# A fused attention and mixture kernel: low parts of second weights on VectorE, three decoded pieces moved into the second mixture, and loads put in another order

## The chip, the cores and the metric

The kernel runs on one core of one Trainium2 chip. The metric is the device time of one execution in microseconds (us). The kernel before took 853.97 us, the median of 3 runs (851.84 to 854.99). The core has five engines with a queue of instructions each: PE (TensorE, matrix products), DVE (VectorE), ACT (ScalarE), POOL (GpSimd) and SP (SyncE, which here only issues DMAs). An instruction waits at the head of its queue until all that it needs is there, and everything behind it in the same queue waits with it.

## The reference

```python
def _attn_ref(q, k, v, beta):                 # 4 batches, 8 heads, 768 tokens, 48 wide
    k_n = k / (np.linalg.norm(k, axis=-1, keepdims=True) + 1e-06)
    state = zeros(B, H, D, D)
    for t in range(S):
        y[:, :, t] = einsum('bhd,bhde->bhe', q[:, :, t], state)
        v_old = einsum('bhde,bhd->bhe', state, k_n[:, :, t])
        state = state + bt * einsum('bhd,bhe->bhde', k_n[:, :, t], vt - v_old)

def _moe_ref(x, w_gate, w_output_gate, w1, w2):   # 3072 tokens, 384 wide, 8 experts of 1024
    e_idx = argmax(x @ w_gate); gate_w = softmax(x @ w_gate)[e_idx]
    eom = 1 / (1 + exp(-(x @ w_output_gate)))
    for e in range(8):
        out[mask] = gate_w * eom[:, e] * (maximum(x[mask] @ w1[e], 0) @ w2[e])

def _moe2_ref(x, w1, w2, w3, w_out):              # hidden width 768
    return maximum(maximum(x @ w1, x @ w2), x @ w3) @ w_out
```

The attention's output is the first mixture's input, and the first mixture's output that of the second.

## The kernel before

**Attention.** The 768 tokens of a sequence go in 24 steps of 32. A step needs the inverse of a triangular 32x32 matrix for each batch and head. Inverses are made by DVE for four steps at a time, six sets in all, by row updates (`inv_step`: a product at L239 and a sum at L245 for each of two halves); `inv_n1` to `inv_n3` prepare a set (square norms, ACT's logarithm and exponentials, DVE's reciprocal at L216, POOL's product of Z at L218), `inv_end` and `inv_store` write it to memory as `td`. In each step the chain then loads the inverse T (`loadT`, L302, the tile TT) and the keys and values (`load32`, L294, the tile kv), POOL scales the values (`vscale`, L308), and PE multiplies (L340 pU, L360 pS). The output x is stored to `xd` (L384). Step by step the tokens' experts are also found, counted (L433 cum) and written as lists into `tab` by POOL's scatters (`r_s`, L474). All of it is written out by hand in one order; times in steps such as `s.RT`, `s.RD` and `s.LT` say between which steps units of loading are put.

**First mixture.** Ten runs, each with the tokens of one expert: runs 0 to 3 of 256 tokens (experts 0 and 1 in parts), runs 4 to 9 of 440, 416, 404, 388, 380 and 368. A run gathers token rows by POOL (`gather`, L837) through a list `ids` (L821), transposes them on PE (`xpose`, L852), multiplies by the first weight (`m1`, tile ph), takes the maximum with zero on ACT (L888), multiplies by the second weight (`o1`, tile po) and stores y into `x2` (L904). `place` (L829) copies a run's list into one list `ctab`. Every product in full precision is three products of high and low parts: `mm3` (L864) of the weight's, tokens' or hidden values' high part (a cast on ACT) and low part (value less high part: L856, L889). For a weight, loaded by `raws` (L679), `split` makes the casts (L695) and the low parts (L696); its last argument is the engine of the low parts, DVE (V) or POOL (G). A first weight is split in three pieces of 128x1024, a second weight in four of 128x768. In a run k from 3 to 8 the next expert's weights are split.

**Second mixture's weights.** They come as 24 pieces of 384 columns of 64-bit words, in six for each of the four weights, the output weight last. Decode (`units`) loads a piece (L600), ACT squares (L606), DVE makes high and low parts in seven steps (L607 to L613), and SP stores them (L603) into `wd`; `load_parts(n)` (L704) loads a whole weight's parts. `pieces` chains the units so that a piece's load is issued within the piece before and its store within the piece behind it; `NP` says how many pieces a run takes.

**Second mixture.** Six blocks of 512 tokens: `m2f` (tile pm) makes three products and their maximum (L937) for each sixth of the hidden width, `o2` (tile pz) the output, which POOL scatters to its place (L950).

**Order.** In `run` each unit has a due time as a share of a run; they are sorted by it and issued in that order, which fixes every engine's queue. `s.values` reads 17 numbers of the table into SP's registers (L804), 15 for starts and experts and 2 for `s.st`, the starts of run 2's and 3's lists.

Of the kernel before, what the change touches and what calls it, by code (L numbers as in the profile page):

```python
# [8 lines left out]
F32 = mybir.dt.float32  # L9
F32R = mybir.dt.float32r  # L10
BF16 = mybir.dt.bfloat16
I32 = mybir.dt.int32
# [21 lines left out]
class Attn:  # L34
# [9 lines left out]
    def __init__(s, ctx, tc, psum, big, hp, gp, kqt, knv, bt, wgt, xd, tab, ctab, cum, ident, wrm, x2):  # L44
        s.tc, s.nc, s.psum, s.big, s.hp, s.gp = tc, tc.nc, psum, big, hp, gp
        nc = tc.nc
        s.kqt, s.knv, s.btd, s.wgtd, s.xd, s.tab, s.ctab, s.cum = kqt, knv, bt, wgt, xd, tab, ctab, cum
        s.ident, s.wrm, s.ones, s.x2 = ident, wrm, wrm[:, 0:128], x2
        s.NI = 24
        s.NP = 12  # L50
        s.NSL = 6
        s.RLB = "m"
        s.XB, s.xTs, s.RLK = 1, {}, 0
        s.CUT = 0.95
        s.NL = 4
        s.NA = 20
        s.LATE = 0.4
        s.W = (0, 1, 0)
        s.END = 13
        s.TU, s.TB, s.MF = (22.92, 22.95, 22.97), "TRT", 2  # L60

        s.BUD = (5.0, 5.6, 4.6, 5.0)

        s.ORD = {0: 0, 1: 14, 2: 36, 3: 50, 4: 66, 5: 80}
        s.prep = (2.8, 2.2, 1.5, 0.6)
        cp = s.cp = ctx.enter_context(tc.tile_pool(name="acst", bufs=1))
        s.p2 = ctx.enter_context(tc.tile_pool(name="ap2", bufs=2))
        s.dr = ctx.enter_context(tc.tile_pool(name="adr", bufs=1, space=DRAM))
        nc.scalar.preload_act_table_set("natural_log_exp_and_others")
        s.chain = False  # L70
        s.RT, s.RD, s.LT = (15.4, (15.9, 0.3), (17.4, 0.35), (20.7, 0.25)), 0.5, ((18.2, 0.45), (19.3, 0.35), (23.0, 0.05))
        s.KQT, s.AT, s.Gd, s.kv, s.TT, s.x, s.inv = {}, {}, {}, {}, {}, {}, {}

    def consts(s):
# [413 lines left out]
    def run(s, pre, tail):  # L488
# [12 lines left out]
        s1 = s.ORD[1]  # L501
        for f in merge(B[:s1 // 3], [A[4], A[5]]) + merge(B[s1 // 3:s1 // 2], [A[6], A[7]]):
            f()
        s.inv_load(1)
        for f in (s.inv_n1, s.inv_n2, s.inv_n3):
            f(1)
        for f in merge(B[s1 // 2:], [A[8], lambda: s.load32(0), A[9], s.empty, A[10], lambda: s.load32(1), A[11], lambda: s.inv_load(2)] + A[12:s.NA]):
            f()
        s.inv_end(0)
        s.warm(8, s.inv[0]["tt"])  # L510
# [114 lines left out]
class Moe:  # L625
# [179 lines left out]
                                skip_runtime_bounds_check_because="the tables keep them in range")  # L805

    def values(s):
        s.at = [0] + [s.value(s.irow, 24 + k, 0, COLS - r.n) for k, r in enumerate(s.runs) if k]
        s.ex |= {2 + k: s.value(s.irow, 34 + k, 0, 7) for k in range(6)}
        s.st = [s.value(s.irow, 40 + k, 0, s.PART) for k in range(2)]  # L810

    def start(s, r):

# [262 lines left out]
        a.r_p(q)  # L1076
        m(7)

    NP = {2: 2, 3: 2, 4: 4, 5: 4, 6: 4, 7: 4, 8: 4}

    def pieces(s):

        N = s.dec.N
        rd = [s.work[:, j * 2 * N:(j + 1) * 2 * N] for j in range(2)]
        wd = [s.work[:, (j + 1) * 4 * N:(j + 2) * 4 * N] for j in range(2)]
        u = [s.dec.units(rd[j % 2], wd[j % 2]) for j in range(len(s.dec.pieces))]
        out = []
        for j, (ld, us, st) in enumerate(u):
            nxt = [u[j + 1][0]] if j + 1 < len(u) else []
            prev = [u[j - 1][2]] if j else []  # L1090
            out.append(([ld] if j == 0 else []) + us[:2] + nxt + us[2:4] + prev + us[4:] + ([] if nxt else [st]))
        return out

    def run(s, a):
        nc = s.nc
        A, V, G = nc.scalar, nc.vector, nc.gpsimd
        s.raw = [s.p.tile([128, 3072], F32, name=f"raw{n}") for n in range(2)]
        s.work = s.p.tile([128, 12 * s.dec.N], I32, name="work")
        pieces = s.pieces()
        last = len(s.runs) - 1  # L1100
# [10 lines left out]
        for k, r in enumerate(s.runs):  # L1111

            us = []
            o = [lambda c=c: s.o1(k, c) for c in range(3)]
            x = [lambda c=c: s.xpose(k + 1, c) for c in range(3)] if k < last else []
            if k == 0:
                us += [(0, load(1, 1)), (0, lambda: a.r_s(range(4)))]
                us += [(0.01, lambda: s.xtiles(1, "1")), (0.02, x[0]), (0.2, o[0]), (0.3, x[1]), (0.5, o[1]), (0.6, x[2]), (0.7, o[2])]
                us += [(0.01, lambda: s.count(24)), (0.3, s.table), (0.4, s.table2), (0.65, s.table3), (0.8, s.values), (0.85, lambda: (s.ids(2), s.ids(3))), (0.9, lambda: rows(2))]
            else:  # L1120
                us += spread([lambda f=f: s.m1(k, f) for f in range(8)], 0, 0.5)
                us += list(zip((0.51, 0.65, 0.82), o))
                if k < last:
                    us += [(0.495, lambda: s.xtiles(k + 1, f"{k + 1}"))] + list(zip((0.5, 0.52, 0.66) if k > 1 else (0.66, 0.83, 0.84), x))
            if k == 1:
                us += spread(s.split(1, 1, A, V), 0.05, 0.4)
                us += [(-0.01, lambda: [s.ids(j) for j in range(4, 10)])]
            if k:

                free = [j for j in range(len(s.rowsets) - 6) if max(s.rowsets[j][0] - 1, 1) == k]  # L1130
                for j in free:
                    t = 0.0 if s.rowsets[j][0] < 2 else 0.845 if k == 1 else 0.665
                    us += [(t, lambda n=s.rowsets[j + 6]: s.gather(*n))]
            if k == 1:
                us += [(0.4, load(2, 0)), (0.5, pieces[0].pop(0))]
            if 3 <= k < last:
                us += spread(s.split(k - 1, 0, A, V), 0.05, 0.35) + spread(s.split(k - 1, 1, A, G), 0.5, 1)
                if k < last - 1:
                    us += [(0.6, load(k, 0))]
            if 4 <= k < last or k == 2:  # L1140
                us += [(0.15, load(max(k - 1, 2), 1))]
            if 2 <= k < last:
                us += [(0.02, lambda j=j: s.place(j)) for j in ({2: [0, 1, 2], 3: [3]}.get(k, [k]))]
                d = []
                for _ in range(s.NP.get(k, 0)):
                    d += pieces.pop(0)
                us += spread(d, 0.0, 1)
            if k == last - 1:
                us += [(0.51, lambda: s.load_parts(0))]
            if k == last:  # L1150
                us += [(0, lambda: s.place(last)), (0.01, lambda: s.load2(0)), (0.02, lambda: s.load_parts(1))]
                us += [(0.5, lambda: s.load2(1)), (0.505, lambda: s.load_parts(2))]
                us += spread([lambda c=c: s.split2(0, c) for c in range(3)], 0.6, 0.9)
            for _, u in sorted(us, key=lambda u: u[0]):
                u()
            s.ystore(k)
        s.load_parts(3)
        for b in range(6):
            us = [lambda f=f: s.m2f(b, f) for f in range(6)]
            if b < 5:  # L1160
                us += [lambda c=c: s.split2(b + 1, c) for c in range(3)]
            for u in us:
# [99 lines left out]
```

## Time and profile before

| | |
|---|---|
| median of 3 runs | 853.97 us (851.84 to 854.99) |
| profiled execution, own time | 854.27 us |
| its span | 852.6 us |
| PE busy | 746.0 us, 87% of the span |
| DVE busy | 479.7 us, 56% |
| ACT busy | 297.8 us, 35% |
| POOL busy | 279.3 us, 33% |
| DMA | 110.28 MB, 129 GB/s in the mean |

The profile is one execution. Busy shares are means over stages with different limits, so they are to be read by stage: the prologue (to about 70 us), the attention chain (to about 283), the ten runs of the first mixture (from 279 to 542, runs 4 to 9 from 369) and the second mixture (to 847). In the rows, "start us, us, engine line op out<-in xcount" is a time from the span's start, a duration, and a count of equal instructions grouped into one row; the brackets at the end say how long the engine was idle just before and what ended that. SPq and POOLq are these engines' own queues, where an issue that waits is shown as one wait. PEclk is the granted clock of TensorE, 1.00 being the higher of its two levels (2.4 GHz) and 0.50 the lower (1.2 GHz).

### The profile page before, as it was taken

The page shows a single profiled execution, that of the slowest core. Times are in us where ns is not written, and L with a number is a line of the kernel's source. Part 1 is how long each engine was busy: PE and PEld are TensorE (multiplying, and loading weights), DVE is VectorE, ACT ScalarE, POOL GpSimd, SP SyncE. Part 2 cuts the span into 40 slices and gives each one's busy share as a digit, 9 for nine tenths or more (in the row PEclk, how much of TensorE's full clock was granted, in tenths as well). Part 3 has the DMA queues.
Part 4 walks back from the last instruction along what each step waited for, and adds up shares of the span by engine and source line. Part 5 has one row for each costly group of instructions (what it writes and reads, how often), then busy time and mean ns, then how long its engine had stood idle before and what let it go on. Part 6 is the DMA issues. An engine that isn't in the chain of part 4 may idle for free. (4 is left out here: it accounts for less than half of the span.)

```text
span 852.6 us, 20332 instructions
## 1 busy us (share of the span) xinstructions
PE 746.0 (87%) x8506; PEld 635.6 (75%) x8517; DVE 479.7 (56%) x1140; ACT 297.8 (35%) x675; POOL 279.3 (33%) x346
## 2 busy tenths in 40 slices
PE   6656877778774897999999999999999999999996
PEld 4544554555552896989899889889888898988886
DVE  3898989985543453688889996132331323223130
ACT  2213576664331332454455353212121121212111
POOL 5766456522575631165455322001001010100101
PEclk7557799999786998999999999999999999999998
DMA  8795544547616126667887684901001020000001
GB/s 233 168 231 128 142 120 121 101 133 184 179 21 171 65 72 190 206 209 246 256 272 254 240 300 164 400 22 56 18 16 60 1 75 1 28 10 1 37 1 40
DMA packets 85756, 110.28 MB, mean 129 GB/s; under 512 B 53860, under 2 KB 67115, under 8 KB 82971
## 3 DMA queue, kind: packets, MB, share of 16 engines
q1 hardware_dynamic: 57259, 87.08, 32.9%
q10 hardware_dynamic: 19360, 11.42, 5.7%
q0 software_dynamic: 9040, 10.42, 4.1%
q8 instruction: 69, 1.13, 0.6%
q14 instruction: 28, 0.23, 0.1%
HBM read 79.53 MB, written 29.36 MB: 128 GB/s over the span
## 5 line engine op out<-in xcount | busy, mean ns | idle before, releaser
L864 PE MATMUL pm<-xhm,wm 128*128 128x512 f32 x648 | 204.9, 396 | 1.4 <-DMA wm<-wd 1.4
L937 DVE TENSOR_TENSOR work<-work,pm 128x512 f32<-128x512 f32 x72 | 49.5, 688 | 186.5 <-PE pm L864 186.5
L864 PEld LDWEIGHTS pm<-xhm,wm 128*128 128x128 f32 x648 | 121.9, 188 | 30.7 <-DMA wm<-wd 1.9
L864 PE MATMUL pm<-xlm,wm 128*128 128x512 f32 x324 | 128.2, 396 | 0.0
L950 POOL DMA_INDIRECT out_dram<-work,idm x24 | 23.7, 986 | 303.3 <-ACT work L949 289.0
L939 ACT CAST hmh<-work 128x512 fp32r<-128x512 f32 x36 | 22.4, 622 | 155.8 <-DVE work L937 155.8
L239 DVE TENSOR_TENSOR zt<-Z 128x30 f32<-128x30 f32 (+14 forms) x219 | 74.3, 378 | 3.2 <-POOL Z L218 2.6
L864 PE MATMUL pz<-wm,hmh 128*128 128x384 f32 x320 | 73.7, 334 | 0.0
L864 PEld LDWEIGHTS pm<-xlm,wm 128*128 128x128 f32 x324 | 61.0, 188 | 14.3
L348 ACT COPY Ubd<-pU 32x192 f32<-32x192 f32 x148 | 45.8, 309 | 66.4 <-PE pU L340 63.5
L245 DVE TENSOR_TENSOR Z<-Z,zt 128x30 f32<-128x30 f32 (+14 forms) x219 | 66.2, 342 | 0.0
L164 PE MATMUL pg<-KQT 48*32 48x64 f32 x1536 | 40.3, 293 | 21.6 <-DMA KQT<-in_kqt_dram 17.6
L837 POOL DMA_INDIRECT xg<-xd,ids x32 | 44.4, 1387 | 44.5 <-PE pt L852 29.0
L360 PE MATMUL pS<-Ubd,kv 128*48 128x192 f32 x368 | 44.2, 378 | 16.6 <-ACT Ubd L348 12.1
L864 PEld LDWEIGHTS pz<-wm,hmh 128*128 128x128 f32 x320 | 57.2, 188 | 0.5
L164 PEld LDWEIGHTS pg<-KQT 48*32 48x32 f32 x1536 | 34.5, 152 | 28.5 <-issue 15.8
L360 PEld LDWEIGHTS pS<-Ubd,kv 128*48 128x48 f32 x368 | 24.5, 140 | 36.7 <-ACT Ubd L348 23.3
L367 ACT COPY Sbd<-pS 48x384 f32<-48x384 f32 x72 | 34.0, 472 | 14.2 <-PE pS L360 13.1
L899 ACT COPY y<-po 128x256 f32<-128x256 f32 (+6 forms) x30 | 13.3, 443 | 72.3 <-PE po L864 72.3
L864 PE MATMUL pz<-wm,hml 128*128 128x384 f32 x112 | 37.4, 334 | 0.0
L308 POOL TENSOR_TENSOR kv<-kv,TT 128x384 f32<-128x384 f32 x20 | 20.8, 1040 | 46.1 <-DMA TT<-td 23.7
L888 ACT ACTIVATE hh<-ph 128x440 fp32r<-128x440 f32 (+5 forms) x48 | 24.0, 502 | 33.9 <-PE ph L864 33.6
(303 smaller groups left out, 1664.3 us busy)
## 6 DMA issues: line engine op xcount, KB each, us to landing
raw<-in_w_dram SPq DMA_DIRECT2D x13, 1536.0 KB, 10.6
kv<-in_knv_dram SPq DMA_DIRECT2D x24, 384.0 KB, 4.6
wd<-work SPq DMA_DIRECT2D x24, 384.0 KB, 5.1
wm<-wd SPq DMA_DIRECT2D x8, 1152.0 KB, 7.9
KQT<-in_kqt_dram ACTq DMA_DIRECT2D x20, 448.0 KB, 4.8
xd<-x SPq DMA_DIRECT2D x24, 192.0 KB, 5.1
r<-in_w_dram SPq DMA_DIRECT2D x9, 512.0 KB, 7.0
raw<-x SPq DMA_DIRECT2D x6, 768.0 KB, 4.9
```

The lines of the kernel that those rows point to most:

```text
L164: nc.tensor.matmul(ps[b * 32:b * 32 + 32, o:o + 64], kq[:, 0, :], kq.rearrange("p k t -> p (k t)"), start=True, stop=True, tile_position=( ...
L239: nc.vector.tensor_mul(t, Z[:, a:e, m].unsqueeze(2).to_broadcast([128, e - a, n]), Z[:, m, m + 1:].unsqueeze(1).to_broadcast([128, e - a, n]))
L245: nc.vector.tensor_add(Z[:, a:e, m + 1:], Z[:, a:e, m + 1:], t)
L348: nc.scalar.copy(dst, src)
L360: nc.tensor.matmul(s.pS[q][j * 64:j * 64 + 48, g2 * 192:g2 * 192 + 192], s.kv[i][:, 0, h, :], s.Ubd[h // 4][:, h % 4, :], start=(i == 0 an ...
L367: nc.scalar.copy(dst, src)
L837: s.nc.gpsimd.indirect_dma_start(t[0:r.ct], None, s.xd[0:2049] if k < 2 else s.xd, bass.IndirectOffsetOnAxis(s.gid[k][0:r.ct, c, 0:1], 0))
L864: s.nc.tensor.matmul(ps, a, b, start=(start and k == 0), stop=(stop and k == n - 1))
L888: nc.scalar.activation(hi, ps, AF.Relu)
L937: nc.vector.tensor_max(m, m, ps)
L939: nc.scalar.copy(hi, m)
L950: nc.gpsimd.indirect_dma_start(s.out, bass.IndirectOffsetOnAxis(i[:, c, 2:3], 0), y, None, bounds_check=3071, oob_is_err=False)
```

## The change

1. In runs 3 to 8 the low parts of the second weight, four of 128x768 in each, are made by DVE instead of POOL (`split(k - 1, 1, A, V)`).
2. The time from which the third weight (the first weight of expert 1) is loaded is 21.8 steps instead of 20.7 (`s.RT`).
3. Runs 5, 6 and 7 decode three pieces instead of four. The last three pieces, all of the output weight, are loaded into the raw weights' tiles and decoded in the first block of the second mixture, one behind each of its first three sixths; the output weight's load (`load_parts(3)`) is issued after the third.
4. In the prologue the preparation of inverse 1 is merged with steps 7 to 13 of inverse 0, so that the reciprocal stands behind step 13 instead of ahead of step 8; products A[8] and A[9] come ahead of its ACT part, and the load of kv for step 1 and the filling of the lists (`empty`) come later.
5. The load of the second weight of expert 1 (`raws(1, 1)`) is three DMAs of 128x1024 instead of one of 128x3072.
6. `values` is cut in two: two register loads, then the lists of runs 2 and 3, then the other fifteen.
7. The first piece's load is issued ahead of run 1's other units instead of in its middle.

```diff
-        s.RT, ... = (15.4, (15.9, 0.3), (17.4, 0.35), (20.7, 0.25)), ...
+        s.RT, ... = (15.4, (15.9, 0.3), (17.4, 0.35), (21.8, 0.25)), ...
...
-        for f in (s.inv_n1, s.inv_n2, s.inv_n3):
-            f(1)
-        for f in merge(B[s1 // 2:], [A[8], lambda: s.load32(0), A[9], s.empty, A[10], lambda: s.load32(1), A[11], lambda: s.inv_load(2)] + A[12:s.NA]):
+        s.inv_n1(1)
+        for f in merge(B[s1 // 2:s1], [A[8], A[9], lambda: s.inv_n2(1), A[10], lambda: s.inv_n3(1)]):
+            f()
+        for f in merge(B[s1:], [lambda: s.load32(0), A[11], lambda: s.inv_load(2), s.empty, lambda: s.load32(1)] + A[12:s.NA]):
             f()
...
     def values(s):
+        s.st = [s.value(s.irow, 40 + k, 0, s.PART) for k in range(2)]
+
+    def values2(s):
         s.at = [0] + [s.value(s.irow, 24 + k, 0, COLS - r.n) for k, r in enumerate(s.runs) if k]
         s.ex |= {2 + k: s.value(s.irow, 34 + k, 0, 7) for k in range(6)}
-        s.st = [s.value(s.irow, 40 + k, 0, s.PART) for k in range(2)]
...
-    NP = {2: 2, 3: 2, 4: 4, 5: 4, 6: 4, 7: 4, 8: 4}
+    NP = {2: 2, 3: 2, 4: 4, 5: 3, 6: 3, 7: 3, 8: 4}
...
-        u = [s.dec.units(rd[j % 2], wd[j % 2]) for j in range(len(s.dec.pieces))]
+        rl = [s.rawi[j][:, 1536:1536 + 2 * N] for j in range(2)]
+        m = sum(s.NP.values())
+        u = [s.dec.units((rd if j < m else rl)[j % 2], wd[j % 2] if j < m else s.work[:, 2560:2560 + 4 * N])
+             for j in range(len(s.dec.pieces))]
...
-            out.append(([ld] if j == 0 else []) + us[:2] + nxt + us[2:4] + prev + us[4:] + ([] if nxt else [st]))
+            out.append(([ld] if j == 0 else []) + (prev if j == m else []) + us[:2] + nxt + us[2:4] + (prev if j < m else []) + us[4:] + ([st] if j >= m else []))
...
-                us += [(0, load(1, 1)), (0, lambda: a.r_s(range(4)))]
+                us += [(0, lambda: [u() for u in s.raws(1, 1, lambda: s.raw[1], 3)]), (0, lambda: a.r_s(range(4)))]
...
-                us += [... (0.8, s.values), (0.85, lambda: (s.ids(2), s.ids(3))), (0.9, lambda: rows(2))]
+                us += [... (0.8, s.values), (0.85, lambda: (s.ids(2), s.ids(3), s.values2())), (0.9, lambda: rows(2))]
...
-                us += [(0.4, load(2, 0)), (0.5, pieces[0].pop(0))]
+                us += [(-0.02, pieces[0].pop(0)), (0.4, load(2, 0))]
...
-                us += spread(s.split(k - 1, 0, A, V), 0.05, 0.35) + spread(s.split(k - 1, 1, A, G), 0.5, 1)
+                us += spread(s.split(k - 1, 0, A, V), 0.05, 0.35) + spread(s.split(k - 1, 1, A, V), 0.5, 1)
...
-        s.load_parts(3)
         for b in range(6):
             us = [lambda f=f: s.m2f(b, f) for f in range(6)]
+            if b == 0:
+                w = [u for p in pieces for u in [lambda p=p: [f() for f in p]]]
+                us = [u for j in range(6) for u in [us[j]] + w[j:j + 1] + ([lambda: s.load_parts(3)] if j == len(w) - 1 else [])]
```

PE's queue holds the same 3413 rows in the same order as before. Line numbers of the changed kernel are up to nine higher.

In SP's queue at the end of the chain, before (r_1 is the third weight, TT and kv belong to the last steps, ids are the lists of runs 0 and 1):

```order
L679 DMA r_1_4598<-in_w_dram 128x1024
L384 DMA xd<-x_4507 128x384
L679 ISA
L679 DMA r_1_4598<-in_w_dram 128x1024
L302 DMA TT_4646<-td_173 128x8x33
L294 DMA kv_4649<-in_knv_dram 128x768
L821 ISA
L821 DMA ids_4711<-tab 128x2x3
```

The same stretch of SP's queue now:

```order
L384 DMA xd<-x_4507 128x384
L302 DMA TT_4643<-td_173 128x8x33
L294 DMA kv_4646<-in_knv_dram 128x768
L824 ISA
L824 DMA ids_4708<-tab 128x2x3
L824 ISA
L824 DMA ids_4710<-tab 128x2x3
L384 DMA xd<-x_4626 128x384
L680 ISA
L680 DMA r_1_4769<-in_w_dram 128x1024
L302 DMA TT_4795<-td_173 128x8x33
L680 ISA
```

All loads of the third weight now stand behind the TT and kv of one more step and behind both lists; the last step's TT is between the first and the second of them.

In SP's queue at the end of run 1 and the start of run 2, before (raw_5232 is the first weight of expert 2, work<-in_ma a piece's load):

```order
L821 DMA ids_5440<-tab 92x4x3
L679 ISA
L679 DMA raw_5232<-in_w_dram 128x3072
L600 DMA work<-in_ma_dram 128x768
L904 REGISTER_ALU
L904 DMA x_77<-y_5591 384x1x256
L829 ISA
L829 DMA ctab<-tab 16x48
```

The same place now, from the end of run 0's store on:

```order
L907 DMA x_77<-y_5277 384x1x256
L601 DMA work<-in_ma_dram 128x768
L824 ISA
L824 DMA ids_5433<-tab 110x4x3
...
L680 DMA raw_5232<-in_w_dram 128x3072
L907 REGISTER_ALU
L907 DMA x_77<-y_5593 384x1x256
...
L832 DMA ctab<-tab 16x48
L601 DMA work<-in_ma_dram 128x768
L680 ISA
```

The first piece's load moved ahead of six list loads and the raw weight; the second piece's, the last DMA but one shown, stays behind the copies into ctab.

In DVE's queue in the second half of run 4 (xl are the low parts of run 5's tokens, work the decode, w_3l the low parts of the second weight of expert 3), before:

```order
L856 TENSOR_TENSOR xl_6287<-pt_0_6288,xh_6286 128x416
L856 TENSOR_TENSOR xl_6287<-pt_1_6327,xh_6286 128x416
L607 TENSOR_SCALAR work<-work 128x384
L608 SCALAR_TENSOR_TENSOR work<-work 128x384
L609 SCALAR_TENSOR_TENSOR work<-work 128x384
L610 TENSOR_SCALAR work<-work 128x384
```

And now:

```order
L859 TENSOR_TENSOR xl_6289<-pt_0_6290,xh_6288 128x416
L697 TENSOR_TENSOR w_3l<-raw_5233,w_3h 128x768
L859 TENSOR_TENSOR xl_6289<-pt_1_6329,xh_6288 128x416
L608 TENSOR_SCALAR work<-work 128x384
L609 SCALAR_TENSOR_TENSOR work<-work 128x384
L610 SCALAR_TENSOR_TENSOR work<-work 128x384
L697 TENSOR_TENSOR w_3l<-raw_5233,w_3h 128x768
```

The four low parts of a second weight now stand among the tokens' low parts and the decode steps of DVE.

## Rows read from the trace of the kernel before

**Rows 1.** Busy us of each engine in two stretches, with granted clock, DMA share, GB/s:
```profile
371.00:542.00 171.00, 164.18 (x915) 156.92 (x915) 144.06 (x221) 78.00 (x138) 70.14 (x38) 1.00 0.76 252
542.00:853.00 311.00, 302.52 (x1408) 258.05 (x1406) 83.47 (x123) 65.74 (x112) 23.67 (x24) 0.99 0.12 41
```
**Rows 2.** Timeline of DVE in the prologue (start, duration, instruction, idle before):
```profile
32.12 0.35 DVE L216 RECIPROCAL vt<-vt 128x32 f32<-128x32 f32 x1 [2.30 <-POOL vt L207]
32.39 0.35 DVE L239 TENSOR_TENSOR zt<-Z 128x92 f32<-128x92 f32 x2
...
33.15 2.47 DVE L239 TENSOR_TENSOR zt<-Z 128x110 f32<-128x110 f32 x2
```
**Rows 3.** Timeline of POOL in the prologue:
```profile
32.92 2.40 POOL L218 TENSOR_TENSOR Z<-Z,vnw 128x1024 f32<-128x1024 f32 x1
```
**Rows 4.** Waits of the queue SP, 230 to 292 us (total, times, longest):
```profile
SPq L679 <- POOL w_0l L696: 20.0, 1, 20.0
```
**Rows 5.** Timeline of POOL at the end of the chain:
```profile
255.29 1.81 POOL L696 TENSOR_TENSOR w_0l<-r,w_0h 128x768 fp32r<-128x768 f32 x1
264.00 0.84 POOL L308 TENSOR_TENSOR kv<-kv,TT 128x384 f32<-128x384 f32 x1 [6.90 <-DMA TT<-td]
```
**Rows 6.** Timeline of the queue SP at the same place:
```profile
258.53 0.47 SPq L302 DMA_DIRECT2D TT<-td  x1
```
**Rows 7.** Timeline of PE at the same place:
```profile
265.60 0.19 PE L452 MATMUL pK<-cum,wrm 128*128 128x32 bf16 x1 [8.81 <-POOL cum L433]
```
**Rows 8.** Timeline of the queue SP, runs 0 to 2:
```profile
310.88 1.07 SPq L821 DMA_DIRECT2D ids<-tab  x2
...
323.72 0.43 SPq L600 DMA_DIRECT2D work<-in_ma_dram  x1
...
325.23 12.53 SPq L829 DMA_DIRECT2D ctab<-tab  x3
337.82 0.56 SPq L600 DMA_DIRECT2D work<-in_ma_dram  x1
```
**Rows 9.** Waits of PE, 312 to 350 us:
```profile
PE pt L852 <- DMA xg<-xd,ids: 2.1, 2, 1.7
```
**Rows 10.** Busy us of each engine in two stretches of runs 2 and 3:
```profile
326.00:339.60 13.60, 8.15 (x54) 7.95 (x52) 4.57 (x12) 2.15 (x7) 0.57 (x1) 0.75 0.58 181
339.60:346.00 6.40, 6.40 (x55) 6.40 (x55) 2.99 (x7) 2.22 (x6) 0.00 (x0) 1.00 0.97 358
```
**Rows 11.** Timeline of ACT, second piece:
```profile
341.36 0.55 ACT L606 ACTIVATE work<-work 128x384 f32<-128x384 f32 x1 [0.22 <-DMA work<-in_ma_dram]
```
**Rows 12.** Transposes on PE from 346 us (duration in ns, first and last start):
```profile
L852 PE MATMUL pt<-ident,xg x2: 272/274/275, 346.7 to 346.9; 128*128 128x128 f32 x2
```
**Rows 13.** Timeline of DVE in run 3:
```profile
360.21 1.93 DVE L612 TENSOR_SCALAR work<-work 128x384 int32<-128x384 int32 x1
```
**Rows 14.** Timeline of POOL in run 3:
```profile
360.09 1.84 POOL L696 TENSOR_TENSOR w_2l<-raw,w_2h 128x768 fp32r<-128x768 f32 x1 [10.46 <-ACT w_2h L695]
```
**Rows 15.** Busy us of DVE, ACT and POOL on the decode's tile alone:
```profile
344.80:350.50 5.70, 3.28 (x7) 0.00 (x0) 0.00 (x0) 1.00 0.49 169
350.50:542.00 191.50, 103.50 (x154) 12.26 (x22) 0.00 (x0) 1.00 0.74 246
```
**Rows 16.** Low parts on DVE (ns minimum, median, maximum; first and last start):
```profile
L696 DVE TENSOR_TENSOR w_1l<-raw,w_1h x4: 947/957/959, 306.4 to 311.5; 128x768 fp32r<-128x768 f32 x4
```
**Rows 17.** Waits of PE, 369 to 543 us:
```profile
PE ph L864 <- DVE hl L889: 4.1, 7, 1.3
PE po L864 <- DVE hh L889: 2.7, 3, 1.4
```
**Rows 18.** Group of PE's first products of the second mixture (busy, mean ns, idle before):
```profile
L864 PE MATMUL pm<-xhm,wm 128*128 128x512 f32 x648 | 204.9, 396 | 1.4 <-DMA wm<-wd 1.4
```
**Rows 19.** DMA issues, KB each and median us to landing:
```profile
wd<-work SPq DMA_DIRECT2D x24, 384.0 KB, 5.1
wm<-wd SPq DMA_DIRECT2D x8, 1152.0 KB, 7.9
```

More of the change, by code (lines that the diff above doesn't have):

```diff
@@ L70, in __init__ @@
         s.chain = False
-        s.RT, s.RD, s.LT = (15.4, (15.9, 0.3), (17.4, 0.35), (20.7, 0.25)), 0.5, ((18.2, 0.45), (19.3, 0.35), (23.0, 0.05))
+        s.RT, s.RD, s.LT = (15.4, (15.9, 0.3), (17.4, 0.35), (21.8, 0.25)), 0.5, ((18.2, 0.45), (19.3, 0.35), (23.0, 0.05))
         s.KQT, s.AT, s.Gd, s.kv, s.TT, s.x, s.inv = {}, {}, {}, {}, {}, {}, {}
@@ L1096, in run @@
         A, V, G = nc.scalar, nc.vector, nc.gpsimd
-        s.raw = [s.p.tile([128, 3072], F32, name=f"raw{n}") for n in range(2)]
+        s.rawi = [s.p.tile([128, 3072], I32, name=f"raw{n}") for n in range(2)]
+        s.raw = [t.bitcast(F32) for t in s.rawi]
         s.work = s.p.tile([128, 12 * s.dec.N], I32, name="work")
@@ L1116, in run @@
             if k == 0:
-                us += [(0, load(1, 1)), (0, lambda: a.r_s(range(4)))]
+                us += [(0, lambda: [u() for u in s.raws(1, 1, lambda: s.raw[1], 3)]), (0, lambda: a.r_s(range(4)))]
                 us += [(0.01, lambda: s.xtiles(1, "1")), (0.02, x[0]), (0.2, o[0]), (0.3, x[1]), (0.5, o[1]), (0.6, x[2]), (0.7, o[2])]
-                us += [(0.01, lambda: s.count(24)), (0.3, s.table), (0.4, s.table2), (0.65, s.table3), (0.8, s.values), (0.85, lambda: (s.ids(2), s.ids(3))), (0.9, lambda: rows(2))]
+                us += [(0.01, lambda: s.count(24)), (0.3, s.table), (0.4, s.table2), (0.65, s.table3), (0.8, s.values), (0.85, lambda: (s.ids(2), s.ids(3), s.values2())), (0.9, lambda: rows(2))]
             else:
```

## The prediction

> **What bounds the kernel now.** I read the busy time of each engine by stage first; the timelines of the chain and of the runs give the bounds of the stages. In the second mixture PE (TensorE) is busy for 302.5 of 311 us [rows 1]: what the change does to other engines can be worth there only the few us that PE waits. In the runs from 371 to 542 us PE is busy for 164.2 of 171 us, so 6.8 us can be had, and DVE (VectorE) for 144 us [rows 1]. Ahead of that the kernel is looser, so I looked in each part of it for the wait that ends last: DVE's and POOL's timelines in the prologue (GpSimd is POOL), the waits of the queue SP in the tail of the attention chain, PE's waits and ACT's (ScalarE's) in runs 0 to 3.
>
> **The inverse's order (prologue).** DVE sat idle for 2.30 us before the reciprocal of inverse 1, waiting for POOL, and just after it a pair of products of the first inverse took 2.47 us, where the pair before took 0.35 [rows 2], beside POOL's 2.40 us product of Z [rows 3]. The chain needs the first inverse, DVE's last work of the prologue, so what DVE loses there PE loses. Now six steps of the first inverse, which need nothing of POOL, stand ahead of the reciprocal, and the 2.30 goes. But POOL's product of Z still follows the reciprocal: it now runs against step 14 and ahead of inverse 1's first step, which needs its result, some 2.4 us of POOL against about 1.5 us of DVE's work before that step. So I take 1.5 us off, between 0 (the wait comes back) and 2.3.
>
> **The third weight's loads (tail of the chain).** One wait rules here: SP stood for 20.0 us, for POOL's low parts of expert 0's second weight, before it could issue the first load of the third weight [rows 4]. The low parts end at 255.29 + 1.81 = 257.1 [rows 5]. The load of T for the last steps but one (TT) was queued behind it and went out at 258.53 [rows 6]; when it had landed, POOL, after 6.90 us of idling, scaled kv at 264.00 [rows 5], and PE began again at 265.60 after 8.81 us without work [rows 7]. The change puts that TT, its kv and the lists (ids) ahead of the blocked load. They land while POOL is still in its low parts, and POOL scales kv at 257.1 instead of 264.0: 6.9 us at most. I take 6.5, as the last step's TT now stands between the loads of the third weight. It is next late: issued after 257.1 and landing some 5.5 us later, as the former did (258.53 to 264.0), it is there near 263, against a need about 6 us after the first scaling at 257.1. It just fits; if not, the gain is given back, at worst all but about 1 us.
>
> **Runs 0 to 3.** PE waited twice for gathered tokens, 2.1 us in all [rows 9], since 17 register loads stand in SP's queue ahead of the lists, which went at 310.88 [rows 8]. Fifteen of them now stand behind the lists: the 2.1 us goes. The greater loss is the first decoded piece. Its load went out at 323.72 [rows 8], behind a raw weight of 1.5 MB; ACT, in order, sat before that piece's square and with it before the activations that PE needs. In the 13.6 us from 326 to 339.6 PE ran 54 matmuls, at a mean granted clock of 0.75; the next 55 took 6.4 us at 1.00 [rows 10]. So this place costs 13.6 - 54 x 0.116 = 7.3 us. With the load issued in run 1, ahead of the long list loads, it goes: 7.3 + 2.1 = 9.4 us at most.
>
> But the second piece's load has not moved. It is behind three copies of the lists (ctab), which held SP for 12.53 us from 325.23, and went at 337.82 [rows 8]; ACT took its square at 341.36, the moment it landed [rows 11]. That square stands in ACT's order behind the last activation of run 2 and ahead of the casts of run 3's tokens. Run 2's products now start 2.1 us earlier and end near 330; PE has some 6 us more (two sets of transposes and output products), and waits from about 336.5 until 0.9 us after the square, which lies between 339.6 (all earlier by 2.1) and 342.5. So PE comes to the third transposes at 341.5 to 343.5, where it now is at 346.9 [rows 12]: 3.4 to 5.4 us gained, of which I put 2 us to a clock that may fall again after the idling, as it did before. I take 2.3 us, from -1.5 (slower) to 9.4. The raw weight in rows of 4 KB changes a transfer that PE does not wait for; I cost it at nothing, and it can at most have a part of the 2.1 us just counted.
>
> **Run 3.** A decode step took 1.93 us on DVE [rows 13] beside POOL's low part of 1.84 us [rows 14], where the mean step of an undisturbed piece takes 3.28 / 7 = 0.47 [rows 15], and a low part that PE's next product needs stood behind it. With the low parts on DVE this collision goes: I take 1.2 us, from 0 to 1.6.
>
> **Runs 4 to 9.** DVE's decode took 103.5 us for 154 operations, 22 pieces; an undisturbed piece took 3.28 us [rows 15], 72.2 for 22. So 31.3 us are stretching, nearly all of it beside POOL's 24 low parts, as in run 3; some 5 of it I leave to the gathers, which stay on POOL. DVE made such a low part itself in 0.957 us [rows 16]. So DVE takes on 24 x 0.957 = 23.0 us, is rid of some 26 us of stretching, and gives 3 x 3.28 = 9.8 us to the second mixture: about 13 us less. PE's waits in these runs are all for DVE, 4.1 + 2.7 = 6.8 us [rows 17], as much as its idle time by stage [rows 1]. I take 6.8 (0 to 6.8): none of the waits, each 1.4 us at most, keeps its cause. Added waits: a low part on DVE waits for ACT's cast, and the low parts of tokens and hidden values stand behind it; DVE's low parts of the first weights are placed in the same way already.
>
> The Trainium skill speaks against this move: "Perfetto Trace Analysis", Optimizing Scalar/DVE Operations, says that with a saturated DVE handing work to ScalarE or even GpSimd may make sense, and this change goes the other way. By that rule DVE would have more to do and the runs would grow, which is the last rival below. The same place adds that the two engines share an SBUF read port, so that moving work between them might not help; rows 13 to 15 agree with that half (1.93 us beside POOL, 0.47 without).
>
> **Second mixture.** PE waited 1.4 us for its weights at the start [rows 18]: their loads are queued on SP behind the stores of decoded pieces, which now end earlier: 1.4 us (0 to 1.4). The three moved pieces lie where DVE is busy for 83.5 of 311 us [rows 1], 27%, so in each 6.5 us that PE gives a sixth of a block about 4.7 are free, and 3.28 fits. The output weight, complete only after the third, is needed when PE begins the first block's output, about 39 us into it. By order the third piece is decoded about 24 us in; 5.1 us for the store and 7.9 for the load [rows 19] make 37: hidden with 2 us to spare, and 1 to 3 us lost if not.
>
> **The sum.** 1.5 + 6.5 + 2.3 + 1.2 + 6.8 + 1.4 = 19.7 us. The profiled execution took 854.27 us (span 852.6), within 0.04% of the median of the three runs, 853.97. 854.3 - 19.7 = 834.6 us.
>
> **Rivals.** *Nothing takes the place of the waits*: the second piece is early too, and each place gives all it has: 2.3 + 6.9 + 9.4 + 1.2 + 6.8 + 1.4 = 28.0, so 826.3 us. For it: the 7.3 us are the longest gap of the runs. Against: three copies still stand before the piece. *The first two places keep their time*: POOL's product meets step 14, and TT and gathers come late behind the third weight's loads, so that the two give 1.0 instead of 8.0: 841.6 us. For it: TT just fits. *DVE's relief does not reach PE*: run 3, runs 4 to 9 and the start of the second mixture (9.4 us) give nothing, as the low parts come on DVE when PE waits: 834.6 + 9.4 = 844.0 us. Against: the stretched operations are where PE waited. *Slower*: the stretching is not POOL's, or comes back with the gathers, and DVE is what runs 3 to 8 go by. Then they lose 23.0 - 9.8 = 13.2 us, and with an assumed 0.3 us of waiting for each cast 20.4, against 10.3 from the first three places: 857 to 864 us. It decides where less than about 3 us of the 31.3 goes. For it: DVE's 144 of 171 us. Against: it has 27 us free there, and rows 13 to 15.
>
> **How the numbers follow.** Forecast 0.60, within 827 to 842; nothing in their place 0.13; the first two places 0.12; no relief 0.08; slower 0.07. The range 822 to 846 leaves out the slower case and little beyond. What this measurement can tell from no change is 0.5%, 4.3 us: 850.0 to 858.5. The first four cases lie below; of the last about half lies above. Allowing for two terms that fail together: faster 0.90, same 0.05, slower 0.05.
>
> **What would show it.** No TT behind SP's long wait, and kv scaled near 257 instead of 264; ACT's first square on time and its second late, with PE waiting before run 3's third transposes; decode steps at 0.47 us in the mean in runs 4 to 8, and no PE wait for DVE over 1 us there; no gap before the first block's output. It is wrong if DVE is busy for longer than before between the same two points of runs 4 to 9, if the second piece's wait is absent or above 8 us, or if PE still idles for 8 us in the tail of the chain.

## The result and the profile after

The changed kernel took 841.91 us, the median of 4 runs (839.51 to 848.06), against 852.9 of 4 runs of the kernel before: a ratio of 0.9859, with a 95% interval of 0.9817 to 0.9902. Run again beside the experiments it took 840.36 us against 853.77, 0.9841 (0.9801 to 0.9881). Forecast were 834.6 us, 19.7 less; 11 to 13.4 less came, so that the time lies within the forecast range of 822 to 846 us with little more than half of the forecast gain.

PE's queue is the same in both kernels, so the start of one and the same PE instruction can be read in both traces, and the difference shows where the time went ("to rows n" below names the rows of the kernel before that a line is to be compared with):

| PE instruction | before, us | after, us | difference |
|---|---|---|---|
| products of the prologue's end | 69.67 | 67.47 | -2.2 |
| first tokens of run 0 transposed | 270.56 | 261.04 | -9.5 |
| first tokens of run 2 transposed | 318.47 | 307.25 | -11.2 |
| last first-weight products of run 2 | 339.39 | 321.83 | -17.6 |
| third transposes of run 3's tokens | 346.74 | 337.66 | -9.1 |
| output products of run 2 | 349.48 | 342.63 | -6.9 |
| run 4 | 400.12 | 391.01 | -9.1 |
| run 5 | 423.49 | 417.94 | -5.6 |
| run 9 | 520.05 | 508.76 | -11.3 |
| second mixture | 800.16 | 787.16 | -13.0 |

It is no smooth gain: 10.7 us are given back between 321 and 343 us, and 3.5 in run 5. Between nearly the same points as in rows 1, runs 4 to 9 and the second mixture (busy us of each engine as there; the first stretch ends 1.6 us short of the one there):

```profile
362.90:529.10 166.20, 162.23 (x907) 158.71 (x906) 123.39 (x223) 75.86 (x135) 26.44 (x16) 0.98 0.76 251
529.10:839.00 309.90, 303.85 (x1417) 259.49 (x1415) 92.87 (x145) 67.09 (x115) 23.65 (x24) 0.99 0.14 45
```

DVE is busy for 123.4 us instead of 144.1, POOL for 26.4 instead of 70.1. But PE is idle for 4.0 us of these runs, not for none, and its clock is no longer 1.00. DVE, ACT and POOL on the decode's tile alone, to rows 15:

```profile
342.40:529.10 186.70, 64.98 (x133) 10.56 (x19) 0.00 (x0) 0.98 0.74 246
```

19 pieces took 65.0 us, 3.42 each against 4.70: the stretching is gone. The prologue, DVE's and then POOL's timeline (to rows 2 and 3):

```profile
36.54 0.35 DVE L216 RECIPROCAL vt<-vt 128x32 f32<-128x32 f32 x1
...
37.69 2.56 DVE L239 TENSOR_TENSOR zt<-Z 128x240 f32<-128x240 f32 x2
```
```profile
37.40 2.47 POOL L218 TENSOR_TENSOR Z<-Z,vnw 128x1024 f32<-128x1024 f32 x1
```

DVE's idling has gone, and POOL's product still costs one pair of DVE's products, now of step 15. In the tail of the chain, the queue SP, then POOL, then PE (to rows 4 to 7):

```profile
248.85 0.99 SPq L824 DMA_DIRECT2D ids<-tab  x2
...
251.94 0.35 SPq L680 DMA_DIRECT2D r<-in_w_dram  x1
```
```profile
250.11 1.80 POOL L697 TENSOR_TENSOR w_0l<-r,w_0h 128x768 fp32r<-128x768 f32 x1
251.87 0.84 POOL L308 TENSOR_TENSOR kv<-kv,TT 128x384 f32<-128x384 f32 x1
```
```profile
253.47 0.18 PE L452 MATMUL pK<-cum,wrm 128*128 128x32 bf16 x1 [3.33 <-POOL cum L433]
```

POOL scales kv in the moment when its low parts end, as forecast; PE's idling there falls from 8.81 to 3.33 us, not to about 2. Runs 0 to 3, the queue SP, ACT, and then all of PE's waits from 300 to 545 us (to rows 8, 9, 11 and 17):

```profile
300.76 1.76 SPq L824 DMA_DIRECT2D ids<-tab  x2
307.59 0.67 SPq L907 DMA_DIRECT2D x<-y  x1
...
320.48 12.42 SPq L832 DMA_DIRECT2D ctab<-tab  x3
332.95 0.58 SPq L601 DMA_DIRECT2D work<-in_ma_dram  x1
```
```profile
336.35 0.54 ACT L607 ACTIVATE work<-work 128x384 f32<-128x384 f32 x1 [12.86 <-DMA work<-in_ma_dram]
```
```profile
PE pt L855 <- DVE xl L859: 8.4, 1, 8.4
PE po L867 <- DVE hh L892: 3.5, 2, 3.4
PE pt L855 <- DMA xg<-xd,ids: 3.4, 3, 1.6
```

The wait for the first piece is gone, and a longer one for the second stands before run 3's third transposes: ACT is held for 12.9 us by the square of the piece whose load went at 332.95, behind the copies. Of the 12.42 us of the three copies SP stood for 7.0 waiting for the copy before:
```profile
SPq L832 <- DMA ctab<-tab: 7.0, 2, 6.1
```
Of PE's waits above, the second entry is new. Where it is, by the queue SP, DVE and PE in run 5:

```profile
395.36 0.34 SPq L601 DMA_DIRECT2D work<-in_mb_dram  x1
395.90 0.36 SPq L680 DMA_DIRECT2D raw<-in_w_dram  x1
396.76 0.57 SPq L604 DMA_DIRECT2D wd<-work  x1
```
```profile
411.77 0.56 DVE L609 SCALAR_TENSOR_TENSOR work<-work 128x384 int32<-128x384 int32 x1 [4.30 <-DMA wd<-work]
```
```profile
412.89 0.71 PE L867 MATMUL po<-hh,w_3h 128*128 128x416 f32 x1 [3.36 <-DVE hh L892]
```

With three pieces in a run instead of four their units lie further apart, and the store of a piece falls behind the raw weight's load, 1.5 MB, which before was behind it. DVE may not write the next but one piece until that store has landed; the last low parts of run 5's hidden values stand behind DVE's wait. After both waits PE runs at the lower clock for a while (PEclk 0.50 in the third column from the right):

```profile
337.50:342.50 5.00, 4.84 (x23) 4.84 (x24) 3.84 (x10) 0.84 (x3) 1.95 (x2) 0.50 0.97 344
412.50:418.00 5.50, 5.11 (x17) 4.81 (x18) 4.93 (x10) 1.73 (x3) 0.00 (x0) 0.50 0.34 111
```

At the second mixture's start the wait is gone (to rows 18), and none stands before the first block's output:

```profile
L867 PE MATMUL pm<-xhm,wm 128*128 128x512 f32 x648 | 204.7, 395 | 0.0
```

### The profile page after: what moved, and what is told of

Read it like the earlier page. It is cut to its first block, busy times and chain, and to the rows that moved or that the text cites. A ratio compares the mean times of both kernels' runs of the same rounds, so it can differ in the third digit from the quotient of the medians.

```text
span 839.6 us, 20331 instructions
## 1 busy us (share of the span) xinstructions
PE 742.9 (88%) x8506; PEld 635.5 (76%) x8517; DVE 471.0 (56%) x1164; ACT 297.2 (35%) x675; POOL 228.5 (27%) x322
## 5 line engine op out<-in xcount | busy, mean ns | idle before, releaser
L245 DVE TENSOR_TENSOR Z<-Z,zt 128x30 f32<-128x30 f32 (+14 forms) x219 | 69.0, 355 | 0.0
L859 DVE TENSOR_TENSOR xl<-pt,xh 128x256 fp32r<-128x256 f32 (+6 forms) x27 | 14.0, 520 | 42.2 <-ACT xh L858 33.2
```

Of the source, the lines that this page charges most:

```text
L245: nc.vector.tensor_add(Z[:, a:e, m + 1:], Z[:, a:e, m + 1:], t)
```

## The experiments

All start from the changed kernel; the diffs are cut to the terms that change. Ratios are to the kernel before, on the same chip; 0.001 is 0.85 us. Their intervals are about 0.0035 to each side, so that differences of less than some 4 us between two of them rest on the traces. The last column compares medians, of three chips: e4, e5, e6 and e9 ran on a second, e7, e8, e10 and e11 on a third. By the ratios the differences come out up to 2.2 us otherwise (e5 +9.0, e9 -10.9, e11 -8.6).

| kernel | median us | ratio (95%) | against 840.36 |
|---|---|---|---|
| changed kernel, again | 840.36 | 0.9841 (0.9801 to 0.9881) | |
| e1 copies behind the second piece | 841.77 | 0.9864 (0.9825 to 0.9902) | +1.4 |
| e2 store ahead of the raw load | 834.80 | 0.9786 (0.9747 to 0.9825) | -5.6 |
| e3 both | 837.89 | 0.9801 (0.9759 to 0.9843) | -2.5 |
| e4 first piece's load back | 842.71 | 0.9866 (0.9819 to 0.9913) | +2.4 |
| e5 low parts back on POOL | 850.93 | 0.9946 (0.9914 to 0.9978) | +10.6 |
| e6 third weight's loads back | 844.96 | 0.9898 (0.9864 to 0.9933) | +4.6 |
| e7 inverse's order back | 845.39 | 0.9902 (0.9872 to 0.9931) | +5.0 |
| e8 rows and register loads back | 835.21 | 0.9791 (0.9759 to 0.9822) | -5.2 |
| e9 store ahead, copies spread | 827.68 | 0.9713 (0.9668 to 0.9757) | -12.7 |
| e10 four pieces again | 840.05 | 0.9846 (0.9816 to 0.9875) | -0.3 |
| e11 e9, both pieces loaded early | 833.99 | 0.9740 (0.9695 to 0.9785) | -6.4 |

The theory: each part does what it should, and two places give it back, the loads behind the copies on SP and the store behind the raw load. The rival: the gains were too small to begin with.

**The changed kernel again.** 

> The changed kernel itself once more, as the base for the three runs beside it. If the profiled execution was typical, PE again waits about 8 us for DVE's low parts of run 3's tokens (behind ACT's square of the second piece) and about 3.4 us in run 5, and the time is 840 to 844 us.

 It was so: 7.8 us before the third transposes, 4.2 us for DVE in run 5. It is also a second profile of the same kernel, and shows how far one profile can be trusted: by its differences, -9.3 at run 0's first transposes, -8.8 at run 2's output products and -12.1 at run 9, runs 0 to 3 lose 0.5 us, where the first profile loses 2.7, and PE waits for no gathered tokens from 295 us on, where the first waits 3.4.

**e2, the store.** Diff:
```diff
-us += [(0.15, load(max(k - 1, 2), 1))]
+us += [(0.18 if s.NP.get(k) == 3 else 0.15, load(max(k - 1, 2), 1))]
```


> Changed kernel, with the raw second weight's load of runs 5, 6 and 7 issued behind the store of a decoded piece, as it stands before the change, instead of ahead of it. Theory A (with three pieces in a run the units lie further apart, so the 1.5 MB load got ahead of the store; DVE's next piece waits for that store with the last hidden values of run 5 behind it): the 4.3 us wait of DVE and PE's 3.4 us wait in run 5 go, with the half clock after them, 4 to 6 us less than the changed kernel. Rival B (the store is late because all the DMA engines are full in run 5, whatever the order): the wait stays and the time is the same within 1 us.

 5.6 us less, and no wait of PE is listed from 340 us to the end of run 9. In the trace the gain from run 4 (400.12 before) to run 9 (520.05) is 9.4 us, where the changed kernel has 2.2. Theory A holds. Between the points of rows 1 (371.00 and 542.00 before):
```profile
359.45:519.87 160.42, 160.42 (x915) 158.03 (x914) 123.41 (x223) 75.84 (x135) 26.32 (x16) 1.00 0.78 264
```
PE is never idle there, and the stretch is 10.6 us shorter than before, more than the 6.8 us that PE idled: PE's busy time itself fell, from 164.2 to 160.4 us at a granted clock of 1.00 in both. Why it fell is not shown.

**e1 and e3, the copies behind the second piece.** Diff:
```diff
-us += [(0.02, lambda j=j: s.place(j)) for j in ({2: [0, 1, 2], ...
+us += [(0.12 if k == 2 else 0.02, lambda j=j: s.place(j)) for j in ({2: [0, 1, 2], ...
```


> Changed kernel, with the three list copies of run 2 issued behind the second piece's load instead of ahead of it. Theory A (the copies hold SP for 12.4 us, the load behind them holds ACT, and with it PE for 8.4 us and then half a clock for about 2 us more): the wait is gone, 9 to 10.5 us less than the changed kernel, about 832. Rival B (the place is bound by something else as well, the gathered tokens of run 3 or the second weight's load, which only stood in the shadow): PE waits there for that instead, and less than 3 us is won.

> Changed kernel with both moves. If the two places are independent their gains add: 13 to 16 us less than the changed kernel, 826 to 829 us, faster than both kernels. If the time won at the first is waited for at the second (a shared DMA transfer or queue), the sum is smaller by several us.


Neither gain of theory A came: e1 is no faster, and e3 is no faster than e2 alone (837.89 against 834.80 us, within the intervals). What took the gain is not what the expectations had named for that case. e1's queue SP, its ACT and its PE's waits from 318 to 360 us:
```profile
324.97 1.40 SPq L601 DMA_DIRECT2D work<-in_ma_dram  x1
326.58 10.68 SPq L832 DMA_DIRECT2D ctab<-tab  x3
337.69 0.19 SPq L680 DMA_DIRECT2D raw<-in_w_dram  x1
337.99 0.37 SPq L601 DMA_DIRECT2D work<-in_ma_dram  x1
```
```profile
347.45 0.54 ACT L607 ACTIVATE work<-work 128x384 f32<-128x384 f32 x1 [6.89 <-DMA work<-in_ma_dram]
```
```profile
PE ph L867 <- DVE h L892: 6.6, 1, 6.6
PE pt L855 <- DVE xl L859: 2.2, 1, 2.2
```
The wait for the second piece fell from 8 to 2.2 us, and the third piece, now behind the copies and a raw weight, cost 6.6. My theory was too narrow: not the second piece is late but whatever stands behind three copies that wait for each other.

**e9, the copies spread.** Diff (with that of e2):
```diff
-us += [(0.02, lambda j=j: s.place(j)) for j in ({2: [0, 1, 2], 3: [3]}.get(k, [k]))]
+us += [(0.02, lambda j=j: s.place(j)) for j in [k]] if k > 3 else \
+      [(t, lambda j=j: s.place(j)) for t, j in {2: [(0.12, 0), (0.6, 1)], 3: [(0.02, 2), (0.5, 3)]}[k]]
```


> Changed kernel with the store ahead of the raw load in runs 5 to 7 and the list copies of run 2 spread out: the first behind the second piece's load, the second in the middle of run 2, the third at the start and the fourth in the middle of run 3, so that none waits on SP for the one before it. Theory A (copies that wait for each other hold SP, and whatever load stands behind them becomes the late one: with the copies behind the second piece it was the third piece): no wait over 3 us in runs 2 and 3, 6 to 9 us less than with the store alone, about 827. Rival B (the DMA queue itself is full there: two raw weights of 1.5 MB and the pieces behind them): the pieces still land late, less than 3 us won.

 827.68 us, 7.1 less than e2 and 12.7 less than the changed kernel (6.2 and 10.9 by the ratios): the fastest of all. Its queue SP at that place, and all of PE's waits from 300 to 545 us:
```profile
316.81 1.25 SPq L601 DMA_DIRECT2D work<-in_ma_dram  x1
318.27 1.10 SPq L832 DMA_DIRECT2D ctab<-tab  x1
319.63 0.39 SPq L680 DMA_DIRECT2D raw<-in_w_dram  x1
320.13 0.67 SPq L601 DMA_DIRECT2D work<-in_ma_dram  x1
```
```profile
PE pt L855 <- DVE xl L859: 3.9, 1, 3.9
PE pt L855 <- DMA xg<-xd,ids: 1.4, 1, 1.4
```
Theory A, as widened: without the waiting copies the third piece's load goes at 320 us, ahead of where the second's was. The 3.9 us that are left are more than the 3 I named.

**e11, the second piece earlier still.** Diff, to e9:
```diff
-us += [(-0.02, pieces[0].pop(0)), (0.4, load(2, 0))]
+us += [(-0.02, pieces[0].pop(0)), (-0.015, pieces[0].pop(2)), (0.4, load(2, 0))]
```


> The kernel with the store ahead of the raw load and the copies spread out, and with the second piece's load issued right behind the first's in run 1, ahead of the list loads and the raw weight. Theory A (what is left before run 3's transposes, 3.9 us in the run before, is this load behind 1.5 MB of raw weight): the wait goes, 3 to 5 us less than 827.7. Rival B (run 3's gathered tokens or the third piece are next late within 1 us): less than 1.5 us.

 It is not faster than e9, if anything slower (the intervals overlap). Its profiled execution was its slowest, 836.71 us, so only the place of its wait is read: 7.7 us for the third piece, one of the two that rival B named. That piece's load went at 330.82, 1.1 us behind a raw weight's load at 329.76, and ACT took its square at 344.89. That the load ahead of it made it late was not tried.

**e4, the first piece.** Diff:
```diff
-us += [(-0.02, pieces[0].pop(0)), (0.4, load(2, 0))]
+us += [(0.4, load(2, 0)), (0.5, pieces[0].pop(0))]
```


> Changed kernel, with the first piece's load back in the middle of run 1 (behind the list loads and the raw weight). Theory A (the end of the place is set by the loads behind the list copies, at about 336 us, and the early first piece only moves PE's waiting from run 2's products to run 3's transposes): the first square is late again by some 5 us, the wait before the third transposes shrinks by as much, and the time stays within 2 us of the changed kernel's 840. Rival B (each late piece costs its own time, as in my sum): 5 to 8 us slower.

 +2.4 us, about 4 to each side. PE's waits from 300 to 350 us:
```profile
PE ph L867 <- DVE h L892: 12.0, 1, 12.0
PE pt L855 <- DMA xg<-xd,ids: 3.0, 2, 1.7
```
The wait is 12.0 us at the first piece and none at the third transposes, against 8.4 there: it moved, as theory A says. But rival B's 5 us are not ruled out by the time, and e4's trace loses 5.9 us from run 0's first transposes to run 2's output products, where the two profiles of the changed kernel lose 2.7 and 0.5: the early load may have been worth a few us of its own.

**e8, rows and register loads.** Diff:
```diff
-(0, lambda: [u() for u in s.raws(1, 1, lambda: s.raw[1], 3)])
+(0, load(1, 1))
-(0.8, s.values), (0.85, lambda: (s.ids(2), s.ids(3), s.values2()))
+(0.8, lambda: (s.values2(), s.values())), (0.85, lambda: (s.ids(2), s.ids(3)))
```


> Changed kernel, with the raw weight of run 0 loaded in rows of 12 KB again and all 17 register loads ahead of the lists of runs 2 and 3. My sum had 2.1 us for the lists and nothing for the rows. Theory A (the lists wait for the last scatter's landing, not for the register loads, and the end of the place is set by the loads behind the copies): within 1.5 us of the changed kernel. Rival B (15 register loads of 0.3 us stand on the way): gathers of run 2 come 4 us later, 2 to 4 us slower.

 Neither: 5.2 us faster. Its queue SP:
```profile
302.55 1.59 SPq L824 DMA_DIRECT2D ids<-tab  x2
304.25 1.20 SPq L907 DMA_DIRECT2D x<-y  x1
...
329.69 0.57 SPq L601 DMA_DIRECT2D work<-in_ma_dram  x1
```
In both kernels the lists go about 4 us after POOL issued the last scatter into their table (296.84 to 300.76 in the changed kernel, 298.42 to 302.55 here). But the store behind the lists goes only at 307.59 in the changed kernel, since fifteen register loads stand between, and here at 304.25: the register loads ran while that scatter was under way. So this part of the change made SP later at all that follows. The two edits were undone together; that the rows have no share was not tried apart. Against the repeated changed kernel's trace about 3.5 us are gained between run 2's first transposes and the end of run 3. As much is gained in run 5, which the edit does not touch: PE's stall there was 3.1 us instead of 4.2 and the granted clock stayed at 1.00, where it was 0.50 from 411.5 to 418.3 us in the other. So only the first half can be put down to the edit.

**e5, POOL.** Diff:
```diff
-spread(s.split(k - 1, 1, A, V), 0.5, 1)
+spread(s.split(k - 1, 1, A, G), 0.5, 1)
```


> Changed kernel, with the second weights' low parts back on POOL in runs 3 to 8 (three pieces in runs 5 to 7 kept). Theory A (POOL's low parts stretch DVE's decode, and that is what PE waited for): decode steps beside them take 1 to 2 us again, PE waits for DVE's low parts in runs 4 to 8, 6 to 8 us slower than the changed kernel. Rival B (with fewer pieces DVE has slack, and the stall in run 5 behind a store goes when DVE is slower): within 3 us of the changed kernel.

 +10.6 us, 9.0 by the ratios, more than theory A named. Its decode's tile and PE's waits in the same runs:
```profile
344.60:540.50 195.90, 93.34 (x133) 10.50 (x19) 0.00 (x0) 0.98 0.70 235
```
```profile
PE po L867 <- DVE hh L892: 8.0, 3, 5.0
PE ph L867 <- DVE hl L892: 2.5, 4, 1.1
PE po L867 <- DVE h L892: 1.2, 1, 1.2
```
4.91 us a piece against 3.42: POOL's low parts are the stretching, and theory A holds. DVE's wait for the store in run 5 is there as well (4.2 us), so the difference is not that stall.

**e10, four pieces.** Diff (the output weight's load and the last store are issued as before the change):
```diff
-NP = {2: 2, 3: 2, 4: 4, 5: 3, 6: 3, 7: 3, 8: 4}
+NP = {2: 2, 3: 2, 4: 4, 5: 4, 6: 4, 7: 4, 8: 4}
```


> Changed kernel, with four pieces in runs 5, 6 and 7 again and none in the second mixture (the output weight is then loaded ahead of it). Theory A (three pieces put the raw weight's load ahead of the store and cost the stall in run 5, more than the 9.8 us of DVE's work moved away were worth to PE): 2 to 6 us faster than the changed kernel, no wait of DVE for a store over 2 us. Rival B (DVE with the low parts and all the pieces is too full): PE waits for DVE in runs 5 to 7, 3 to 8 us slower.

 The time is the changed kernel's, which is neither theory's. PE's waits from 355 to 545 us:
```profile
PE ph L867 <- DVE hl L892: 0.6, 1, 0.6
PE po L867 <- DVE hh L892: 0.3, 1, 0.3
PE pm L867 <- DMA wm<-wd: 0.2, 1, 0.2
```
The stall in run 5 is absent, and DVE with all its pieces is not too full: rival B is out. From run 4 to run 9 its trace gains 7.5 us, against 2.2 in the changed kernel and 9.4 in e2; this profile is some 4 us behind the changed kernel's at run 0, with the same code up to there. So by the traces the move of three pieces was worth about 2 us with the store in place, and cost more than that as it was made; both rest on single profiles, and the medians show neither.

**e6 and e7.** Diff of e6, and of e7:
```diff
-(21.8, 0.25)
+(20.7, 0.25)
```
```diff
-s.inv_n1(1)
-for f in merge(B[s1 // 2:s1], [A[8], A[9], lambda: s.inv_n2(1), A[10], lambda: s.inv_n3(1)]): ...
+for f in (s.inv_n1, s.inv_n2, s.inv_n3):
+    f(1)
```


> Changed kernel, with the third weight's loads back at 20.7 steps. Theory A (the TT behind SP's wait for POOL's low parts held kv and PE): SP's wait has the TT behind it again, PE waits about 8 us in the tail, 6 to 9 us slower than the changed kernel. Rival B (what it loses in the tail it has back before the lists are read, since POOL's scatters and the register loads set the start of the runs): within 3 us.

> Changed kernel, with the preparation of inverse 1 back ahead of steps 7 to 13 of inverse 0. Theory A (DVE's idling before the reciprocal is the chain's loss): DVE waits about 2.3 us there again, the chain begins about 2 us later, and as nothing behind it waits for anything but the chain, the time is 1.5 to 2.5 us above the changed kernel's 840.4. Rival B (the tail's wait for the gathered tokens and lists takes it up): within 0.5 us of the changed kernel.


e6 is 4.6 us slower, between the two theories' bounds; the time can't tell them apart. PE's wait in its tail:
```profile
PE pK L452 <- POOL cum L433: 11.3, 2, 9.4
```
So theory A's wait is back: in the twelve other profiles since the change, all with the late loads, PE waits there for 3.3 us at most.

e7 is 5.0 us slower, more than its theory gave; DVE's idling is back:
```profile
32.39 0.35 DVE L216 RECIPROCAL vt<-vt 128x32 f32<-128x32 f32 x1 [2.30 <-POOL vt L207]
```
In its trace the chain runs 2.5 us later at 200 us than in the repeated changed kernel's, and 3.1 us at the first transposes of run 0. The remaining 2 us are within the intervals.

## Why the prediction was right or wrong, point by point

*The inverse's order*: forecast 1.5 us, 2.2 in the trace, 5.0 by e7 (about 4 to each side). Right; POOL's product did meet DVE's next steps, but at one pair of products, as before, and DVE did not wait.

*The third weight's loads*: forecast 6.5, 7.3 in the trace between the prologue and run 0, 4.6 by e6 (about 4 to each side). The mechanism was right to the moment: kv is scaled when POOL's low parts end. The size is less certain: between the same two points the twelve profiles with this edit gain from 3.1 to 10.1 us (6.1 in the mean), and e6's, without it, 2.9.

*Runs 0 to 3*: forecast 2.3 gained, -1.5 at worst, and 2.7 were lost from run 0's first transposes to run 2's output products (-9.5 to -6.9): 1.7 gained ahead of run 2's first transposes, 4.4 lost behind them. The repeated profile loses 0.5 and those of e2, e5, e6, e7 and e10, which leave this place as it is, 1.9 to 4.4; none gains. This is the step that failed. The first piece gave 6.4 of 7.3 us, and the second piece's wait was foreseen, but I put its square between 339.6 and 342.5 on the old time scale; it came at 336.35 + 11.2 = 347.5. I had moved SP's queue along with PE. It does not follow PE: from the last scatter's landing on it is one chain, lists, register loads, list loads, raw weight, copies. And *"fifteen of them now stand behind the lists: the 2.1 us goes"* was wrong twice. In the kernel before, the lists went 5.0 us behind the last scatter's issue (305.86 to 310.88), now 3.9: they waited for the scatter, and the register loads had cost them about 1 us; PE's waits for tokens are 3.4 us in one profile and none in the other. And the loads, now behind the lists, put some 5 us on that chain (e8). The half clock that I allowed 2 us took about 2.2.

*Run 3 and runs 4 to 9*: forecast 1.2 + 6.8 = 8.0; 4.4 in the trace (-6.9 to -11.3), 3.3 in the repeated one. The mechanism was right: e5 puts the low parts at 10.6 (about 4 to each side), the decode went from 4.70 to 3.42 us a piece, and DVE is busy for some 20 us less, where I had 13. The size was too small, since I held PE's 6.8 idle us to be all that could be had: in e2's trace the same rows gain 12.0 (-10.2 to -22.2). What I missed is that three pieces change the due times of all their units, and so the order of a store and a raw load on SP. It cost 5.6 us by e2, so that the 4.4 are the sum of a larger gain and a loss that I had not seen. The shift stands in the order of SP's queue and could have been read ahead; I read that queue for the chain's tail and runs 0 to 2 alone, and cost the move of three pieces only at its new place.

*Second mixture*: forecast 1.4, 1.7 in the trace. The moved pieces are hidden.

*The Trainium skill's advice the other way* ("Perfetto Trace Analysis", Optimizing Scalar/DVE Operations): DVE was the busiest engine but PE in these runs and took work from POOL, and the kernel is 9 to 10.6 us faster for it than without (e5). Here the measurement decides: what counts is that POOL's work cost DVE more (about 31 us of stretching) than the same work on DVE itself (24 x 0.957 = 23.0 us).

*Rivals*: the slower one did not come about; DVE's relief did reach PE; the first two places gave what they should in the trace. The time of 841.9 us stands near that of the second rival, by another cause. Of the signs of being wrong one came, narrowly: the second piece's wait is above 8 us (8.4, and 7.8 in the repeated profile); and a PE wait for DVE of 3.4 us stands where none over 1 us was to be. That the time still lies in the range is in part luck: the trace gains 13.0 us, with 5.0 missing in runs 0 to 3 and 3.6 in runs 3 to 9, and nothing else in the sum failed.

## What to carry to other kernels

When a wait is removed, follow the queue it stood in to the next load that an in-order engine needs, and time that load by what the queue itself waits for, not by the engine that you sped up. Copies that wait for each other on a queue of loads make whatever follows late, so moving one load ahead of them only chooses the next victim: spread them. When units are spread over a stretch by their count, changing the count moves each of them past its neighbours; compare the order of every queue, not only of the engine that the change is about.

## What the runs showed of the hardware that was not expected

An int32 step with one SBUF input, 0.35 us alone, took 1.93 beside POOL's low part; without POOL's low parts the mean piece is 3.42 us against 3.28 undisturbed, so the gathers that stay on POOL cost the decode 0.14 us a piece, 2.7 us in 19, half of the 5 I had left to them (the six decode steps that took over 0.7 us all ran beside a gather). A store of 384 KB issued 0.9 us behind a raw weight's load (396.76 against 395.90) was waited for until 411.77, 15.0 us, where the median store of the kernel before lands after 5.1 us [rows 19].
